# K of the first unit ahead of the query weights on the load queue of a decode attention kernel

## The chip, the core and the metric

The kernel runs on one core of a Trainium2 chip. The metric is the device time of one execution in microseconds: the median of 3 runs of the kernel before is 1936.8 us (1936.79 to 1936.99). The core has TensorE (PE, matmuls; its weight loads are shown as PEld), VectorE (DVE), ScalarE (ACT), GpSimd (POOL) and SyncE (SP), which here does nothing but issue DMAs. The DMAs run on 16 DMA engines. TensorE and the others work on the on-chip memory SBUF; matmul results go to PSUM.

## What is computed

Two attention blocks, A and B, of the same sizes, each with its own inputs; the outputs are put side by side. One query token, batch 2, 32 heads of 192, a cache of 8192 keys, a model width of 640, all in bf16.

```python
B, Sq, D = 2, 1, 640
Hq, Hkv, Sk, Dh = 32, 32, 8192, 192        # rep = 1
q = (x @ wq).reshape(B, Sq, Hq, Dh).transpose(0, 2, 1, 3)
scores = einsum("bhqd,bhkd->bhqk", q, k_cache) * Dh ** -0.5
o = einsum("bhqk,bhkd->bhqd", softmax(scores), v_cache)
out = o.transpose(0, 2, 1, 3).reshape(B, Sq, Hq * Dh) @ wo
# concatenate(A's out, B's out) on the last axis
```

Almost all of the data are the caches: 64 K loads and 64 V loads of 6144 KB each.

## The kernel before

**Units.** A unit u (0 to 63) is a pair of heads of one batch entry; units 0 to 31 are block A, 32 to 63 block B. Partition p holds 128 consecutive cache rows of one head, 64 partitions for each of the two heads, so a K or V load is 128 rows of 48 KB, contiguous in DRAM (`ld_kv`, L262). A unit's work has these steps:
- VectorE multiplies K by the query in four chunks (`dve_mul`, L286, profile line L288, signal `("m", u, c)`);
- TensorE sums groups of products with an identity matrix into PSUM, 12 matmuls a chunk (`pe_sum`, L365, `("s", u, c)`); VectorE reduces the rest (L292);
- the maximum over all partitions goes through GpSimd (L269), the exponential through ScalarE (L327);
- TensorE sums V with the weights, 64 matmuls (`pe_pv`, L379, `("pv", u)`); VectorE and ScalarE normalise.

A product buffer is used by every second chunk, so the multiply of chunk c waits for the sums of chunk c - 2.

**Queries.** Before any unit, the queries of all heads are made: `pe_x` (L348) transposes x, `dve_xbc` (L274) copies it out, and `pe_q` (L357) multiplies it with `wq` in 32 steps of 5 matmuls, a step being one pair of heads of both batch entries: steps 0 to 15 belong to block A, 16 to 31 to block B. Step hp signals `("pq", hp)`; VectorE (L278) and ScalarE (L283) copy its result into `qall` and signal `("qx", hp)` and `("qa", hp)`. L430 and L431 let TensorE wait for a block's whole weight, and for the copies of x, ahead of its first step. Every `dve_mul` waits by L440 for its K load and also for step 31 with its copies.

**Buffers.** One SBUF tile, `big`, holds three load buffers (0, 1, 2) and two product buffers. While the queries are made, its part behind buffer 0 holds the two query weights: block A's begins at buffer 1, block B's ends with the product buffers (L184 to L187). Buffer 0 is free of them. The loads are numbered in the order K0, K1, V0, K2, V1, K3, V2 and so on (L211 to L214), and load i goes into buffer i mod 3.

**The load queue.** All loads are issued by SP, in the order of L489 to L502, on one queue. The first three lines issue, with no wait, block A's query weight in two pieces (`wq_cut`, L206: the first 2048 of 30720 columns, 512 KB, then 7168 KB), both x inputs (2.5 KB each) and block B's query weight (7680 KB). Then come the K and V loads. A load waits until the work on the load three places ahead is over (`done`, L483): for a K load that is the last multiply of its unit, for a V load the weighted sum. Three of them have other gates:

```python
for i, (kind, u) in enumerate(loads):
    w = [done(i - NBUF)]
    if i in (1, 2):
        w = [("pq", PPB * i - 1)]
    S_sp.add(ld_kv(kind, u), waits=w)
```

So K0 waits for nothing, K1 for step 15 (its buffer holds block A's weight) and V0 for step 31. K2 waits for `("m", 0, 3)`, V1 for `("m", 1, 3)`, K3 for `("pv", 0)`, V2 for `("m", 2, 3)`, K4 for `("pv", 1)`. After the last unit the output weights are loaded and multiplied (`pe_out`, L407), and the result is stored.

TensorE runs unit u's sums and then the weighted sum of unit u - 1's V in each round of its main loop; for the first rounds this gives the order sums of unit 0, sums of unit 1, weighted sum of unit 0, sums of unit 2, weighted sum of unit 1.

Of the kernel before, what the change touches and what calls it, by code (L numbers as in the profile page):

```python
# [117 lines left out]
def build_kernel(nc, blocks, out):  # L118
    NBLK = len(blocks)
    B, Hn, Sk, Dh = blocks[0]["k"].shape  # L120
# [8 lines left out]
    DC = D // 128  # L129
# [7 lines left out]
    NBUF = 3  # L137
# [3 lines left out]
    BUFE = T * Dh  # L141
# [5 lines left out]
    with ExitStack() as es:  # L147
# [7 lines left out]
        big = sb("big", [128, NBUF * BUFE + 2 * PRODE], BF16)  # L155
# [38 lines left out]
        S_sp = _Stream("sp", sem("s_sp"), reg)  # L194
# [6 lines left out]
        def dsem(k, n=1):  # L201
            reg[k] = (sem("d_" + "_".join(str(i) for i in k)), 16 * n)

        dsem(("x",), NBLK)
        WQ0 = 2048
        wq_cut = [[(0, WQ0), (WQ0, DC * Hn * Dh)], [(0, DC * Hn * Dh)]]  # L206
        for blk in range(NBLK):
            dsem(("wq", blk), len(wq_cut[blk]))
            dsem(("odone", blk))
# [5 lines left out]
        buf = {}  # L215
        bcount = [0] * NBUF
        for i, (kind, u) in enumerate(loads):
            buf[kind, u] = i % NBUF
            bcount[i % NBUF] += 1
            reg[(kind, u)] = (bsem[i % NBUF], 16 * bcount[i % NBUF])  # L220

        bk, b62, b63 = buf["k", LASTU], buf["v", LASTU - 1], buf["v", LASTU]
# [22 lines left out]
        def dma(out_ap, in_ap, k):  # L245
            s = reg[k][0]
            return lambda eng: eng.dma_start(out_ap, in_ap).then_inc(s, 16)  # L247

        def ld_x(blk):
            return dma(x4[B * blk:B * blk + B, :], blocks[blk]["x"][:, 0, :], ("x",))  # L250

        def ld_wq(blk, n):
            lo, hi = wq_cut[blk][n]
            src = blocks[blk]["wq"].rearrange("(j c) n -> j (c n)", c=DC)
            return dma(big[:, wq_off[blk] + lo:wq_off[blk] + hi], src[:, lo:hi], ("wq", blk))
# [6 lines left out]
        def ld_kv(kind, u):  # L262
            hp, b = u // B, u % B
            blk, h = hp // PPB, 2 * (hp % PPB)
            src = blocks[blk][kind][b, h:h + 2].rearrange("s (p t) d -> (s p) t d", p=64)
            return dma(kv[buf[kind, u]], src, (kind, u))

        def pool_ar(u):
            return lambda eng: eng.partition_all_reduce(mg[u % 3][:], mp[u % 3][:], 128, bass.bass_isa.ReduceOp.max)  # L269
# [213 lines left out]
        def done(i):  # L483
            if i < 0:
                return None
            kind, u = loads[i]
            return ("m", u, NCH - 1) if kind == "k" else ("pv", u)

        ld_wq(0, 0)(nc.sync)  # L489
        S_sp.add(ld_wq(0, 1))  # L490
        for blk in range(NBLK):
            S_sp.add(ld_x(blk))
        S_sp.add(ld_wq(1, 0))
        for i, (kind, u) in enumerate(loads):
            w = [done(i - NBUF)]
            if i in (1, 2):
                w = [("pq", PPB * i - 1)]
            S_sp.add(ld_kv(kind, u), waits=w)
# [70 lines left out]
def bass_concat_heads__gqa_block_cached__mha_block_cached__decode_kernel(  # L569
    nc: bass.Bass,  # L570
    A_x: bass.AP,
    A_k_cache: bass.AP,
    A_v_cache: bass.AP,
    A_wq: bass.AP,
    A_wo: bass.AP,
    B_x: bass.AP,
    B_k_cache: bass.AP,
    B_v_cache: bass.AP,
    B_wq: bass.AP,
    B_wo: bass.AP,  # L580
    out: bass.AP,
):
    blocks = [
        dict(x=A_x, k=A_k_cache, v=A_v_cache, wq=A_wq, wo=A_wo),
        dict(x=B_x, k=B_k_cache, v=B_v_cache, wq=B_wq, wo=B_wo),
    ]
    build_kernel(nc, blocks, out)
# [28 lines left out]
```

## Time and profile before

| | |
|---|---|
| median of 3 runs | 1936.8 us |
| span of the profiled execution | 1935.4 us |
| bytes read from DRAM | 836.77 MB, 432 GB/s over the span |
| TensorE busy | 1501.1 us (78%) |
| VectorE busy | 1122.5 us (58%) |
| mean granted clock of TensorE | 0.956 |

The span goes from the first instruction to the last; the time of a run is longer by what lies around them. The median stands 1.4 us above the span of the profiled execution. In the rows of the timeline, the first number is the start from the beginning of the span, the second the time until the end of the last of the merged instructions, then engine, line, operation, written and read names, shapes and count; in brackets stands how long the engine had been idle and what released it. "SPq" rows are DMA issues; where two are merged in one row the last of them ends with the row. In the DMA rows the last number is the median time from issue to landing. Rows of a stretch give its length, the busy time of PE, PEld, DVE, ACT and POOL with counts, then the granted clock of TensorE (1 is full speed), the busy share of the DMA engines and the rate.

### The profile page before, as it was taken

The page shows a single profiled execution, that of the slowest core. Times are in us where ns is not written, and L with a number is a line of the kernel's source. Part 1 is how long each engine was busy: PE and PEld are TensorE (multiplying, and loading weights), DVE is VectorE, ACT ScalarE, POOL GpSimd, SP SyncE. Part 2 cuts the span into 40 slices and gives each one's busy share as a digit, 9 for nine tenths or more (in the row PEclk, how much of TensorE's full clock was granted, in tenths as well). Part 3 has the DMA queues.
Part 4 walks back from the last instruction along what each step waited for, and adds up shares of the span by engine and source line. Part 5 has one row for each costly group of instructions (what it writes and reads, how often), then busy time and mean ns, then how long its engine had stood idle before and what let it go on. Part 6 is the DMA issues. An engine that isn't in the chain of part 4 may idle for free.

```text
span 1935.4 us, 19060 instructions
## 1 busy us (share of the span) xinstructions
PE 1501.1 (78%) x7728; PEld 730.0 (38%) x7729; DVE 1122.5 (58%) x907; ACT 142.4 (7%) x519; POOL 28.5 (1%) x113
## 2 busy tenths in 40 slices
PE   5788878878878878877877877877877877877878
PEld 2334433433433433433433333433333433433434
DVE  4765565565565565565565565565565565565560
ACT  3100000000000000000000000000000000000000
POOL 0000000000000000000000000000000000000000
PEclk9899999999999999999999999999999999999998
DMA  9999999999999999999999999999999999999999
GB/s 423 424 435 437 431 434 437 432 433 437 436 429 436 437 430 435 436 432 433 437 435 431 436 435 430 436 437 430 435 437 430 434 438 435 430 436 436 429 436 394
DMA packets 19754, 836.91 MB, mean 432 GB/s; under 512 B 2200, under 2 KB 2336, under 8 KB 2720
## 3 DMA queue, kind: packets, MB, share of 16 engines
q1 hardware_dynamic: 19744, 836.78, 99.9%
q8 instruction: 6, 0.10, 0.0%
q14 instruction: 4, 0.03, 0.0%
HBM read 836.77 MB, written 0.01 MB: 432 GB/s over the span
## 4 chain that ended last, share of the span: by engine, by line
DMA 49%; PE 28%; DVE 17%; issue 5%; DVEq 0%; SPq 0%; ACT 0%; ACTq 0%
DMA big<-in_B_k_cache_dram 25%; DMA big<-in_A_k_cache_dram 22%; PE ops L379 18%; DVE big L288 15%; PE scps L365 8%; DVE sc L292 2%; DMA big<-in_B_wo_dram 1%; PE scps L357 1%; DMA xw<-in_B_x_dram 1%; PE outps L357 0%; PE ops L371 0%; DVEq L288 0%; DVE qall L278 0%; SPq L247 0%; PE scps L407 0%
## 5 line engine op out<-in xcount | busy, mean ns | idle before, releaser
L288 DVE TENSOR_TENSOR big<-big,qall 128x6144 bf16<-128x6144 bf16 x256 | 852.8, 3351 | 526.6 <-DMA big<-in_B_k_cache_dram 278.7
L365 PE MATMUL scps<-big,ident 128*128 128x512 bf16 x3072 | 771.8, 408 | 401.1 <-DVE big L288 398.7
L379 PE MATMUL ops<-big,pb 128*34 128x384 bf16 x4096 | 676.8, 326 | 0.0
L365 PEld LDWEIGHTS scps<-big,ident 128*128 128x128 bf16 x3072 | 301.1, 104 | 865.1 <-DVE big L288 491.0
L379 PEld LDWEIGHTS ops<-big,pb 128*34 128x34 bf16 x4096 | 395.5, 98 | 258.7
L292 DVE TENSOR_REDUCE sc<-scps 128x32 f32<-128x512 f32 x256 | 175.8, 687 | 192.5 <-PE scps L365 192.5
L318 ACT ACTIVATE nb<-mg 64x1 f32<-64x1 f32 x128 | 25.8, 201 | 1706.8 <-POOL mg L269 1706.1
L327 ACT ACTIVATE pb<-sc,nb 64x128 bf16<-64x128 f32 x128 | 55.8, 436 | 7.8
L269 POOL PARTITION_ALL_REDUCE mg<-mp x64 | 25.7, 402 | 1857.9 <-DVE mp L298 1857.9
L298 DVE TENSOR_REDUCE mp<-sc 64x1 f32<-64x128 f32 x128 | 35.9, 280 | 8.3
L312 ACT ACTIVATE qall<-o_sum,rc 2x192 f32 (+1 forms) x64 | 29.0, 453 | 20.7 <-DVE o_sum L309 19.1
L309 DVE TENSOR_TENSOR o_sum<-ops,o_hi 2x192 f32<-2x192 f32 x64 | 22.1, 345 | 7.7
L357 PE MATMUL scps<-big,xw 128*128 x120 | 23.2, 351 | 2.2 <-DVE xw L274 2.2
L327 ACT ACTIVATION_READ_ACCUMULATOR pb<-sc,nb 64x1 f32 x128 | 23.7, 185 | 0.0
L306 DVE COPY o_hi<-ops 2x192 f32<-2x192 f32 x64 | 22.3, 349 | 2.0
L303 DVE RECIPROCAL rc<-ops 2x1 f32<-2x1 f32 x64 | 10.0, 156 | 21.3 <-PE ops L379 19.4
L278 DVE CAST qall<-scps 64x192 f32 x48 | 17.0, 355 | 6.5 <-PE scps L357 4.5
L283 ACT ACTIVATE qall<-scps 64x192 f32 x48 | 15.6, 324 | 30.1 <-DVE qall L278 27.8
L348 PE MATMUL oTps<-ident,xw 4*128 4x4 bf16 x5 | 0.4, 178 | 21.7 <-DMA xw<-in_B_x_dram 21.7
L357 PEld LDWEIGHTS scps<-big,xw 128*128 128x128 bf16 x120 | 12.4, 103 | 11.4 <-issue 5.2
L371 PEld LDWEIGHTS ops<-ones,rs 128*2 128x2 f32 x128 | 5.5, 82 | 26.9 <-issue 26.9
L407 PE MATMUL outps<-big,oT 128*2 128x320 bf16 x96 | 9.5, 375 | 5.6 <-DMA big<-in_A_wo_dram 5.6
(36 smaller groups left out, 67.6 us busy)
## 6 DMA issues: line engine op xcount, KB each, us to landing
big<-in_A_k_cache_dram SPq DMA_DIRECT2D x32, 6144.0 KB, 28.9
big<-in_A_v_cache_dram SPq DMA_DIRECT2D x32, 6144.0 KB, 27.9
big<-in_B_k_cache_dram SPq DMA_DIRECT2D x32, 6144.0 KB, 29.4
big<-in_B_v_cache_dram SPq DMA_DIRECT2D x32, 6144.0 KB, 28.2
big<-in_B_wq_dram SPq DMA_DIRECT2D x1, 7680.0 KB, 37.2
big<-in_A_wo_dram SPq DMA_DIRECT2D x1, 7680.0 KB, 30.1
big<-in_A_wq_dram SPq DMA_DIRECT2D x1, 7168.0 KB, 20.2
big<-in_B_wo_dram SPq DMA_DIRECT2D x1, 4640.0 KB, 30.4
```

What stands on the lines that cost most here:

```text
L269: return lambda eng: eng.partition_all_reduce(mg[u % 3][:], mp[u % 3][:], 128, bass.bass_isa.ReduceOp.max)
L288: return lambda eng: eng.tensor_tensor(prod[c % 2], t[:, c * TC:(c + 1) * TC, :], qall[:, S_dve.at(u), :].broadcast_to([128, TC, Dh]), ALU ...
L292: return lambda eng: eng.tensor_reduce(sc[u % 3][:, c * TC:(c + 1) * TC], scps[(u * NCH + c) % 3][:], AXL.X, ALU.add)
L298: ins = eng.tensor_reduce(mp[u % 3][r, s:s + 1], sc[u % 3][r, :], AXL.X, ALU.max)
L306: return lambda eng: eng.tensor_copy(o_hi[:], ops[u % 3][32:34, Dh:QW])
L309: return lambda eng: eng.tensor_tensor(o_sum[:], ops[u % 3][0:2, 0:Dh], o_hi[:], ALU.add)
L312: return lambda eng: eng.activation(qall[0:2, S_act.at(u), :], o_sum[:].unsqueeze(1), ACTF.Identity, scale=rc[u % 3][:])
L318: ins = eng.activation(nb[u % 3][r, :], mg[u % 3][r, s:s + 1], ACTF.Identity, scale=-scale)
L327: ins = eng.activation(dst, sc[u % 3][r, :].rearrange("p (g j a) -> p g a j", j=JB, a=2), ACTF.Exp, bias=nb[u % 3][r, :], scale=scale, acc ...
L357: ins = eng.matmul(qps[hp % NQ][:, 0:QW], xbc[:, blk, c, :], wq_t[blk][:, c, S_pe.at(off, QW, QW)], start=(c == 0), stop=(c == DC - 1))
L365: ins = eng.matmul(scps[(u * NCH + c) % 3][:], ident[:], prod[c % 2][:, :, j * DG:(j + 1) * DG], start=(j == 0), stop=(j == NJ - 1))
L379: ins = eng.matmul(ops[u % 3][0:MP, 0:QW], pb[u % 3][:, j0s:j0s + MP], vv[:, j, :], start=(j == 0), stop=(j == TJ - 1))
```

## The change

The queue's first entries get another order. K0 now goes out first, in two pieces (columns 0 to 2047 and 2048 to 24575 of each partition's row: 512 KB and 5632 KB) by a new function `ld_k0`; then both x loads; then block A's query weight, whole; then block B's, whole. The loop over the loads leaves out entry 0. Buffers, gates of all other loads, and all work on the engines stay as they are. The semaphore of buffer 0 counts K0 as two transfers.

```diff
-        WQ0 = 2048
-        wq_cut = [[(0, WQ0), (WQ0, DC * Hn * Dh)], [(0, DC * Hn * Dh)]]
+        wq_cut = [[(0, DC * Hn * Dh)], [(0, DC * Hn * Dh)]]
+        k_cut = [(0, 2048), (2048, BUFE)]
...
-            bcount[i % NBUF] += 1
+            bcount[i % NBUF] += len(k_cut) if i == 0 else 1
...
+        def ld_k0(n):
+            lo, hi = k_cut[n]
+            src = blocks[0]["k"][0, 0:2].rearrange("s (p t) d -> (s p) (t d)", p=64)
+            return dma(big[:, lo:hi], src[:, lo:hi], ("k", 0))
...
-        ld_wq(0, 0)(nc.sync)
-        S_sp.add(ld_wq(0, 1))
+        assert buf["k", 0] == 0
+        ld_k0(0)(nc.sync)
+        S_sp.add(ld_k0(1))
         for blk in range(NBLK):
             S_sp.add(ld_x(blk))
+        S_sp.add(ld_wq(0, 0))
         S_sp.add(ld_wq(1, 0))
         for i, (kind, u) in enumerate(loads):
+            if i == 0:
+                continue
             w = [done(i - NBUF)]
```

## The prediction

> **What bounds the kernel now.** I read the DMA rows of the page first, then the busy sums.
>
> ```profile
> span 1935.4 us, 19060 instructions
> PE 1501.1 (78%) x7728; PEld 730.0 (38%) x7729; DVE 1122.5 (58%) x907; ACT 142.4 (7%) x519; POOL 28.5 (1%) x113
> DMA  9999999999999999999999999999999999999999
> GB/s 423 424 435 437 431 434 437 432 433 437 436 429 436 437 430 435 436 432 433 437 435 431 436 435 430 436 437 430 435 437 430 434 438 435 430 436 436 429 436 394
> q1 hardware_dynamic: 19744, 836.78, 99.9%
> ```
>
> The 16 DMA engines are busy 99.9% of the span, and the rate is flat. The kernel is one stream of bytes: a microsecond in which the queue is empty is lost for good, and compute costs nothing as long as it gives buffers back in time. By the busy sums, a unit (one of 64) takes 1501.1 / 64 = 23.5 us of TensorE and 17.5 of VectorE. Next, the rate by stretches (columns: length, busy time of PE, PEld, DVE, ACT, POOL, clock, DMA share, GB/s):
>
> ```profile
> 54.10:98.77 44.67, 32.77 (x139) 14.08 (x140) 32.60 (x21) 3.53 (x15) 3.78 (x2) 0.89 0.99 430
> 98.77:127.96 29.19, 25.52 (x139) 12.79 (x136) 17.15 (x14) 1.85 (x7) 0.35 (x1) 1.00 1.02 439
> 300.00:1900.00 1600.00, 1250.45 (x6365) 606.21 (x6363) 942.61 (x718) 102.61 (x387) 19.49 (x55) 0.96 1.00 434
> ```
>
> At 434 GB/s a K or V load (6144 KB, 6.29 MB) takes 14.5 us, so a unit's two take 29.0, some 5 us more than its TensorE work. A lag of compute therefore heals by about 5 us a unit, but what the stream lost before it healed stays lost. So the change must be judged by when each early load is issued against when the load ahead of it ends. These are the issue rows, the times to landing (last number), and, from the view of the issuing line, the largest time to landing:
>
> ```profile
> 0.72 0.88 SPq L247 DMA_DIRECT2D big<-in_A_wq_dram  x2
> 2.30 0.36 SPq L247 DMA_DIRECT2D big<-in_B_wq_dram  x1
> 2.70 37.84 SPq L247 DMA_DIRECT2D big<-in_A_k_cache_dram  x2
> 53.34 0.33 SPq L247 DMA_DIRECT2D big<-in_A_v_cache_dram  x1
> 71.82 0.33 SPq L247 DMA_DIRECT2D big<-in_A_k_cache_dram  x1
> 89.26 0.33 SPq L247 DMA_DIRECT2D big<-in_A_v_cache_dram  x1
> 102.71 0.33 SPq L247 DMA_DIRECT2D big<-in_A_k_cache_dram  x1
> 113.26 0.33 SPq L247 DMA_DIRECT2D big<-in_A_v_cache_dram  x1
> ```
> ```profile
> big<-in_B_wq_dram SPq DMA_DIRECT2D x1, 7680.0 KB, 37.2
> big<-in_A_wq_dram SPq DMA_DIRECT2D x1, 7168.0 KB, 20.2
> big<-in_A_wq_dram SPq DMA_DIRECT2D x1, 512.0 KB, 3.7
> DMA to landing us min/median/max: 3.7/30.3/51.3
> ```
>
> The second weight lands at 2.30 + 37.2 = 39.5. The 51.3 can only be K of unit 0, issued at 2.70 behind everything else: it lands at 54.0, 14.5 after the weight. K of unit 1 follows in the queue, then V0 (53.34), K2 (71.82), V1 (89.26), K3 (102.71), V2 (113.26). The compute side of that stretch:
>
> ```profile
> 24.29 4.98 PE L357 MATMUL scps<-big,xw 128*128 x15 [2.18 <-DVE xw L274]
> 39.20 0.98 PE L357 MATMUL outps<-big,xw 128*128 x5
> 52.34 0.98 PE L357 MATMUL outps<-big,xw 128*128 x5
> 58.65 7.96 PE L365 MATMUL scps<-big,ident 128*128 128x512 bf16 x24 [5.33 <-DVE big L288]
> 102.61 5.61 PE L365 MATMUL scps<-big,ident 128*128 128x512 bf16 x24
> ```
> ```profile
> 55.19 6.63 DVE L288 TENSOR_TENSOR big<-big,qall 128x6144 bf16<-128x6144 bf16 x2 [0.99 <-ACT qall L283]
> 85.89 3.35 DVE L288 TENSOR_TENSOR big<-big,qall 128x6144 bf16<-128x6144 bf16 x1
> 98.77 6.62 DVE L288 TENSOR_TENSOR big<-big,qall 128x6144 bf16<-128x6144 bf16 x2 [5.38 <-DMA big<-in_A_k_cache_dram]
> 127.96 6.63 DVE L288 TENSOR_TENSOR big<-big,qall 128x6144 bf16<-128x6144 bf16 x2 [9.62 <-DMA big<-in_A_k_cache_dram]
> 156.89 6.63 DVE L288 TENSOR_TENSOR big<-big,qall 128x6144 bf16<-128x6144 bf16 x2 [7.68 <-DMA big<-in_A_k_cache_dram]
> ```
>
> Projections run on TensorE from 24.29 without a gap: block A's end at 40.18, block B's at 53.32. The first score multiply starts at 55.19, released by the last query copy, 1.2 us after K0 landed. Units 0 and 1 then run as fast as compute allows (85.89 + 3.35 = 89.24, and V1 goes out at 89.26). At 98.77 VectorE waits for K2's data for the first time, and from there DMA leads.
>
> **The change, part by part.** All rates below are those of these rows.
>
> *The bytes.* The same six transfers go out at the start, in another order. Two go first as pieces and the merged weight saves one, so SP's issue time stays (0.88 us for two). The first piece is 512 KB as before. I cost this at nothing; the stream has no hole to remove there, so a gain is excluded but for the first fill, which the equal first piece keeps. Either way it is below the 0.4 us of one issue.
>
> *The x loads* move behind K0's 14.5 us instead of behind the first weight, so they land around 18 instead of 21.7 (the first row of the next fence), and the transposition and copies up to 24.29 are over some 15 us before a weight is there. That removes 24.29 - 21.4 = 2.9 us (the first weight landed near 1.2 + 20.2) from between weight and projections. Nothing is gained by it, since the second weight sets what follows.
>
> *The second weight* now ends where K0 ended: 54.0. This is the cost. No multiply may start before the last projection (the waits of L440), so K0, there from about 17 us, lies idle. The first weight lands at 21.4 + 14.5 = 35.9; block A's projections take 40.18 - 24.29 = 15.9 us from a cold start, so they end near 51.85. TensorE then waits 2.2 us, starts again at 54.05 and needs 53.32 - 40.18 = 13.1 us at full clock. Does that wait cool the clock?
>
> ```profile
> 21.75 0.35 PE L348 MATMUL oTps<-ident,xw 4*128 4x4 bf16 x5 [21.75 <-DMA xw<-in_B_x_dram]
> 76.92 7.04 PE L365 MATMUL scps<-big,ident 128*128 128x512 bf16 x24 [2.31 <-DVE mp L298]
> 149.75 7.80 PE L379 MATMUL ops<-big,pb 128*34 128x384 bf16 x47
> 160.31 6.65 PE L365 MATMUL scps<-big,ident 128*128 128x512 bf16 x24 [2.76 <-DVE big L288]
> 168.42 2.76 PE L365 MATMUL scps<-big,ident 128*128 128x512 bf16 x12 [1.46 <-DVE big L288]
> 76.90:79.00 2.10, 2.08 (x7) 0.85 (x8) 2.10 (x1) 0.00 (x0) 1.95 (x1) 0.68 1.25 542
> ```
>
> Twenty-four matmuls without a gap took 5.61 us (102.61). After gaps of 2.76 and 2.31 us they took 6.65 and 7.04, so 1.0 and 1.4 more, and the granted clock behind the second was 0.68; after 1.46 us twelve took 2.76, nothing more. The bounds for a gap of 2.2 are 0 and 1.4. I take 1.0, from the gap that follows an unbroken stream (149.75 to 157.55), as here. So the last projection ends at 54.05 + 13.1 + 1.0 = 68.2 instead of 53.32: **compute starts 14.9 us later**, the first multiply near 70.1.
>
> The Trainium skill, "TensorE: Matmul & The Clock Gate", section "What's actually happening", lets the clock fall to half only after an idle window of about 3.4 us; by that a wait of 2.2 us costs nothing. The rows at 76.92 and 160.31 disagree for gaps shorter than that.
>
> *What the shift meets.* Four loads wait for it, and SP issues in order, so each also holds all behind it. An issue into an empty queue lands after a fixed part and its own 14.5: the fixed part is 3.7 us less 1.2 us for 0.52 MB at 434, so 2.5; I keep 1.5 to 3.5 open, since only this one transfer shows it. A load that finds the queue full lands 14.5 after the one ahead.
> - K1 (waits for block A's projections): 51.85 + 17.0 = 68.85, against 54.0 + 14.5 = 68.5 with a full queue. A pause of 0.35.
> - V0 (block B's): 68.2 + 17.0 = 85.2. Before it was 98.77 - 14.5 = 84.3, so 0.9 late.
> - K2 (unit 0's last multiply): 71.82 + 14.9 = 86.7, landing at 103.7, against 98.77: 4.9 late.
> - V1 (unit 1's last multiply): 89.26 + 14.9 = 104.2, landing at 121.2, against 98.77 + 14.5 = 113.3: **7.9 late**.
> - K3 (unit 0's weighted sum): 102.71 + 14.9 + 17.0 = 134.6, but the queue gives 121.2 + 14.5 = 135.7. No new pause.
> - V2: 113.26 + 14.9 + 17.0 = 145.2, against 135.7 + 14.5 = 150.2. None, and the margin grows from here.
>
> These are not added: each holds the earlier ones. The loss is that of V1, that is the shift of 14.9 less the 98.77 - 2.5 - 89.26 = 7.0 us by which V1 was early. Everything after rides on the stream, to the end. Sum: span 1935.4 + 7.9 = 1943.3; the runs' median is 1936.8, 1.4 above the span, so **1944.7 us**.
>
> The same chain can be shorter by what cold clock it holds. Its first 24 matmuls took 7.96 after 5.33 us of idleness, its next 7.04: at most 2.35 + 1.4 = 3.8 of the 34 us, if both were warm. With no cooling of the projections either, the loss is 3.1. The other end: cooling as long as after 5.33 us (2.35) and a fixed part of 3.5 give 7.9 + 1.35 + 1.0 = 10.3.
>
> **The rivals.**
> - *The clock holds through the 2.2 us.* Then the shift is 13.9, the loss 6.9 and the time 1943.7. For it: the gap is a little shorter than any that cooled. Against: 2.31 cooled. This is the result of the skill's rule above.
> - *Only the direct gates count.* If the multiplies of units 0 and 1 make up the delay (a chain of 30 us rather than 34, warm throughout, and a fixed part below 2.5), only V0 is late: 0.9 to 3 us, 1937.7 to 1940. Against: the 5.33 us ahead of the first score sums is the last copies plus a multiply, which the change leaves there.
> - *The stream makes it up, so the kernel is not slower.* The stretch from 98.77 ran at 439 GB/s right after one at 430. If the engines could hold 439, then 8 us would be regained at 5/434 in some 700 us, and the end would stand at 1936.8. It decides from unit 3 on: K would have to land every 28.6 us instead of 29.0. Against: in 1600 us with loads always queued the mean stayed 434.
> - *The lag goes on.* If K3 and V2 also find the queue empty, the loss tends to the whole shift: 1936.8 + 14.9 = 1951.7. Against: a margin of 1.1 us at K3 and 5 at V2.
> - *The change doesn't do what it says:* if multiplies of unit 0 could start on their own query, K0 early would be of use and only V0's 0.9 us would be lost, 1937.7. The trace can't exclude it, because K0's landing and the last copy fall 1 us apart; the list of waits in the code does.
>
> **How the numbers follow.** Cooled clock, 1944.7: 0.48. Warm, 1943.7: 0.25. Lag goes on: 0.09. Only direct gates: 0.08. Made up: 0.07. Not what it says: 0.03. A measurement of this kernel tells a change from none at about 0.2%, 3.9 us. The first three are slower by more than that, and of the direct gates, 0.02: 0.84. Of the made-up case I give 0.04 to faster, since a rate of 439 need not stop at what was lost; the remaining 0.12 is within 0.2%. The range takes the losses from 4.2 to 10.8 us, 1941.0 to 1947.6; below it are the two cases near 1937 and the faster one, above it most of the lasting lag.
>
> **What would show it.** The x matmuls near 18 us and the first projection near 36; a TensorE gap of about 2 us near 52 and a half clock behind it; the first multiply near 70.1; K2 issued near 86.7 and V1 near 104.2; GB/s in the second and third slice down by about 10% and 6%, and the other slices as they are; later K landings 29.0 apart and 7.9 late (156.89 becomes 164.8). A first multiply before 60 would make the whole sum wrong; a first multiply near 70 without the late landings would break the step from shift to loss; rates above 434 later on would bring in the third rival.

## The result and the profile after

| | before | changed |
|---|---|---|
| median of the runs | 1936.89 us (4 runs, 1936.79 to 1937.14) | 1945.92 us (4 runs, 1944.07 to 1947.07) |
| span of the profiled execution | 1935.4 us | 1942.6 us |
| spread of the runs | 0.35 us | 3.0 us |

The ratio is 1.0046 (95% interval 1.0033 to 1.0058): 9.0 us slower at the median, and 7.2 us by the spans of the two profiled executions. The profiled execution of the changed kernel is its fastest run. The prediction was 1944.7, with a range of 1941.0 to 1947.6.

First the page of the changed kernel: span, DMA share and rate in 40 slices, and the load queue.

```profile
span 1942.6 us, 19081 instructions
DMA  9999999999999999999999999999999999999999
GB/s 413 394 419 433 431 435 437 432 430 435 435 434 434 431 435 435 434 434 431 434 436 433 435 430 434 436 434 434 430 435 436 433 433 432 434 437 433 433 432 390
q1 hardware_dynamic: 19744, 836.78, 99.7%
```

The digit row shows nothing: the pauses are too short for a slice of 49 us. The rates show them. The second and third slices fell from 424 and 435 to 394 and 419, by 7% and 4% where about 10% and 6% were forecast. The first fell too, from 423 to 413; it is 413 in e1 below as well, which has the old order, so this does not come from the order. The other slices stay within 7 GB/s. Next the issue rows of the changed kernel (K1, V0, K2, V1, K3), and from the view of the DMA issues, taken for each load alone, the time from issue to landing (last number; in order block B's weight, issued at 2.70, then K1, V0, K2, V1).

```profile
52.50 0.33 SPq L247 DMA_DIRECT2D big<-in_A_k_cache_dram  x1
67.86 0.33 SPq L247 DMA_DIRECT2D big<-in_A_v_cache_dram  x1
85.44 0.33 SPq L247 DMA_DIRECT2D big<-in_A_k_cache_dram  x1
101.64 0.33 SPq L247 DMA_DIRECT2D big<-in_A_v_cache_dram  x1
115.09 0.33 SPq L247 DMA_DIRECT2D big<-in_A_k_cache_dram  x1
```
```profile
big<-in_B_wq_dram SPq DMA_DIRECT2D x1, 7680.0 KB, 51.4
...
big<-in_A_k_cache_dram SPq DMA_DIRECT2D x1, 6144.0 KB, 17.8
...
big<-in_A_v_cache_dram SPq DMA_DIRECT2D x1, 6144.0 KB, 20.2
...
big<-in_A_k_cache_dram SPq DMA_DIRECT2D x1, 6144.0 KB, 19.2
...
big<-in_A_v_cache_dram SPq DMA_DIRECT2D x1, 6144.0 KB, 18.1
```

The second weight lands at 2.70 + 51.4 = 54.1. K1, V0, K2 and V1 all go out only 1.6 to 3.0 us before the load ahead of them lands, with the queue nearly empty, and land at 70.3, 88.1, 104.6 and 119.7. The same view of the kernel before, for K2 (issued 71.82) and V1 (issued 89.26):

```profile
big<-in_A_k_cache_dram SPq DMA_DIRECT2D x1, 6144.0 KB, 26.9
...
big<-in_A_v_cache_dram SPq DMA_DIRECT2D x1, 6144.0 KB, 24.0
```

There K2 landed at 98.7 and V1 at 113.3, so V1 is 6.5 us late in the changed kernel's fastest run. TensorE and VectorE of the changed kernel in the head, the stretch up to the first units:

```profile
18.14 0.35 PE L353 MATMUL oTps<-ident,xw 4*128 4x4 bf16 x5 [18.14 <-DMA xw<-in_B_x_dram]
36.34 4.98 PE L362 MATMUL scps<-big,xw 128*128 x15 [17.85 <-DMA big<-in_A_wq_dram]
51.49 0.98 PE L362 MATMUL outps<-big,xw 128*128 x5
54.48 2.61 PE L362 MATMUL scps<-big,xw 128*128 x15 [2.01 <-ACT qall L288]
66.86 0.98 PE L362 MATMUL outps<-big,xw 128*128 x5
73.17 6.98 PE L370 MATMUL scps<-big,ident 128*128 128x512 bf16 x24 [5.33 <-DVE big L293]
90.55 2.76 PE L370 MATMUL scps<-big,ident 128*128 128x512 bf16 x12 [2.31 <-DVE mp L303]
```
```profile
69.71 6.63 DVE L293 TENSOR_TENSOR big<-big,qall 128x6144 bf16<-128x6144 bf16 x2 [0.99 <-ACT qall L288]
98.26 3.35 DVE L293 TENSOR_TENSOR big<-big,qall 128x6144 bf16<-128x6144 bf16 x1
105.80 6.63 DVE L293 TENSOR_TENSOR big<-big,qall 128x6144 bf16<-128x6144 bf16 x2
134.28 6.63 DVE L293 TENSOR_TENSOR big<-big,qall 128x6144 bf16<-128x6144 bf16 x2 [3.57 <-DMA big<-in_A_k_cache_dram]
163.53 6.63 DVE L293 TENSOR_TENSOR big<-big,qall 128x6144 bf16<-128x6144 bf16 x2 [8.81 <-DMA big<-in_A_k_cache_dram]
```

Here K0 lies ready while TensorE waits 17.85 us for the first weight and 2.01 us ahead of block B's projections (the row names ScalarE, but what came last was the second weight, at 54.1); the first multiply starts at 69.71 instead of 55.19. VectorE is the late one through unit 2 (no DMA wait at 105.80), and K3 at 134.28 is the first load it waits for again. From there the stream leads, 6.3 us behind that of before (127.96), and K4 at 163.53 is 6.6 behind.

### The profile page after: what moved, and what is told of

Same layout as the page of the kernel before. It is cut to its first block, busy times and chain, and to the rows that moved or that the text cites. A ratio compares the mean times of both kernels' runs of the same rounds, so it can differ in the third digit from the quotient of the medians.

```text
span 1942.6 us, 19081 instructions
## 1 busy us (share of the span) xinstructions
PE 1533.7 (79%) x7729; PEld 738.9 (38%) x7729; DVE 1123.0 (58%) x907; ACT 142.3 (7%) x519; POOL 31.6 (2%) x113
## 4 chain that ended last, share of the span: by engine, by line
DMA 47%; PE 32%; DVE 17%; issue 3%; DVEq 0%; SPq 0%; ACT 0%; ACTq 0%
DMA big<-in_B_k_cache_dram 24%; DMA big<-in_A_k_cache_dram 21%; PE ops L384 18%; DVE big L293 15%; PE scps L370 12%; DMA big<-in_A_wq_dram 2%; DVE sc L297 1%; DMA big<-in_B_wo_dram 1%; PE scps L362 1%; PE outps L362 0%; PE ops L376 0%; DVE qall L283 0%; DVEq L293 0%; SPq L247 0%; PE scps L412 0%
## 5 line engine op out<-in xcount | busy, mean ns | idle before, releaser
L370 PE MATMUL scps<-big,ident 128*128 128x512 bf16 x3072 | 804.1, 421 | 362.3 <-DVE big L293 360.0
L370 PEld LDWEIGHTS scps<-big,ident 128*128 128x128 bf16 x3072 | 310.2, 106 | 849.4 <-DVE big L293 446.5
L303 DVE TENSOR_REDUCE mp<-sc 64x1 f32<-64x128 f32 x128 | 35.9, 281 | 8.3
L353 PE MATMUL oTps<-ident,xw 4*128 4x4 bf16 x5 | 0.4, 178 | 18.1 <-DMA xw<-in_B_x_dram 18.1
## 6 DMA issues: line engine op xcount, KB each, us to landing
big<-in_B_wq_dram SPq DMA_DIRECT2D x1, 7680.0 KB, 51.4
```

The costliest lines, as they stand in the source:

```text
L303: ins = eng.tensor_reduce(mp[u % 3][r, s:s + 1], sc[u % 3][r, :], AXL.X, ALU.max)
L370: ins = eng.matmul(scps[(u * NCH + c) % 3][:], ident[:], prod[c % 2][:, :, j * DG:(j + 1) * DG], start=(j == 0), stop=(j == NJ - 1))
```

## The experiments

All diffs are against the changed kernel unless another is named; their code is shortened, and a line of several loads gives the order of issue. Times are medians with the range of the runs; the kernel before, run beside them on the same chip, stood at 1936.78 to 1936.85.

**The pieces without the new order (e1).**

```diff
-ld_k0(0), ld_k0(1), ld_x(0), ld_x(1), ld_wq(0), ld_wq(1)
+ld_wq(0), ld_x(0), ld_x(1), ld_wq(1), ld_k0(0), ld_k0(1)
```

> Queue order of before (block A's weight, x, block B's weight, K0), but with the changed kernel's pieces: block A's weight whole, K0 in 512 KB and 5632 KB. Theory (the late second weight is the cost, the pieces are free): within 0.4 us of the 1936.9 of before, runs within 0.5 us of each other. Rival (the cut of K0 or the whole first weight costs something of its own): above 1938.

1937.52 us (1937.23 to 1937.69, 11 runs) against 1936.81 (1936.54 to 1937.13, 15 runs of the kernel before). Neither expectation held: the order makes nearly all of the loss, but the pieces cost 0.7 us, and the two sets of runs do not overlap. Two more runs share it out.

**One piece at a time (f1, f2), each against the kernel before.**

```diff
 # f1
-wq_cut = [[(0, WQ0), (WQ0, DC * Hn * Dh)], [(0, DC * Hn * Dh)]]
+wq_cut = [[(0, DC * Hn * Dh)], [(0, DC * Hn * Dh)]]
 # f2
-K0 whole, as ld_kv
+ld_k0(0), ld_k0(1), behind both weights
```

> The kernel before with one thing changed: block A's query weight goes out whole instead of in two pieces; K0 stays whole and last. It and f2_k0_cut share out the 0.7 us by which e1_cut_only, which has both, was slower than before. If the whole weight is what costs (a first transfer that fills the empty queue later, or another state of the queue's end): 1937.4 to 1937.7. If not: within 0.25 us of before.

> The kernel before with one thing changed: K0 goes out in two pieces, at its old place behind both weights. If the cut of K0 is what costs the 0.7 us of e1_cut_only: 1937.4 to 1937.7. If not: within 0.25 us of before.

1937.32 (1937.21 to 1937.51) and 1937.11 (1936.97 to 1937.23), against 1936.78: 0.5 and 0.3 us. Both fall short of the 1937.4 expected of a piece that costs the whole 0.7, and both lie beyond the 0.25 of one that costs nothing, so each has some share. The time isn't lost in the head. V1 lands at 113.3 in e1 as before, and the two traces part in the last microseconds, at the last loads of the output weights. The last row of such matmuls, of the kernel before and then of e1:

```profile
1932.15 1.44 PE L407 MATMUL scps<-big,oT 128*2 128x320 bf16 x16 [0.19 <-DMA big<-in_B_wo_dram]
```
```profile
1932.69 1.47 PE L412 MATMUL scps<-big,oT 128*2 128x320 bf16 x16 [0.59 <-DMA big<-in_B_wo_dram]
```

TensorE waits 0.59 us instead of 0.19 for the last bytes. That the cuts leave the 16 engines finishing at more uneven times is a guess; no run shows it.

**The first weight ahead of K0 (e2).**

```diff
-ld_k0(0), ld_k0(1), ld_x(0), ld_x(1), ld_wq(0), ld_wq(1)
+ld_wq(0), ld_x(0), ld_x(1), ld_k0(0), ld_k0(1), ld_wq(1)
```

> Block A's weight first, then x, then K0 in its two pieces, then block B's weight. Block A's projections end near 40 as before and K1 is issued then; the second weight still lands at 54. Theory (only the second weight's landing counts): as slow as the changed kernel or slower, 1944 to 1948, since TensorE now waits about 14 us ahead of block B's projections and starts them at half clock (some 2 us more than after the 2 us gap); V1 is issued between 101 and 106. Rival (K1's late issue, or K0 ahead of everything, is the cost): 1937 to 1938.

1948.85 us (1947.43 to 1949.21, 5 runs), ratio 1.0062 (1.0049 to 1.0076): even slower than the changed kernel, and 0.85 us above the expected 1944 to 1948. TensorE and SP of e2:

```profile
55.05 4.28 PE L362 MATMUL scps<-big,xw 128*128 x15 [16.11 <-DMA big<-in_B_wq_dram]
```
```profile
38.97 0.33 SPq L247 DMA_DIRECT2D big<-in_A_k_cache_dram  x1
105.02 0.33 SPq L247 DMA_DIRECT2D big<-in_A_v_cache_dram  x1
```

K1 goes out at 38.97, 13.5 us sooner than in the changed kernel, and it is of no use, nor is it K0's place ahead of the first weight that costs. Block B's weight still comes behind K0, V1 still goes out late, at 105.02, and after the long wait the projections start at half clock (15 matmuls in 4.28 us instead of 2.61).

**x ahead of everything (e4).** Both x loads first, then as in the changed kernel.

> The changed kernel with both x loads at the head of the queue, ahead of K0. Theory: x is early enough in either place, so the time is that of the changed kernel, 1944 to 1947; the x matmuls move from 18 us to below 6. Rival (the place of the x loads behind K0 matters): below 1943 or above 1948.

1947.94 us (1946.25 to 1948.28, 5 runs). The x matmuls start at 2.92 instead of 18.14, and nothing is gained. The median lies 0.9 us above the expected 1944 to 1947, and just short of the rival's 1948. Part of that is the start of the stream: K0's first piece now goes out at 1.40 instead of 0.72, and the second weight lands at 54.7 instead of 54.1.

**How much may go ahead (d1, d2, d3).** Only the first n columns of K0 go ahead; the rest follows block B's weight.

```diff
-k_cut = [(0, 2048), (2048, BUFE)]
+k_cut = [(0, n), (n, BUFE)]          # n = 6144, 12288, 18432 of 24576
-ld_k0(0), ld_k0(1), ld_x(0), ld_x(1), ld_wq(0), ld_wq(1)
+ld_k0(0), ld_x(0), ld_x(1), ld_wq(0), ld_wq(1), ld_k0(1)
```

> Only the first quarter of K0 (1536 KB, 3.6 us) goes ahead of x and the weights; the rest of K0 follows block B's weight. Theory (threshold: compute shifts by the bytes ahead of the second weight, and the first 6 to 7 us of the shift are free): 1936.9, runs within 0.5 us. Rival (the loss is in proportion to the bytes moved ahead): 1939.1.

> The first half of K0 (3072 KB, 7.25 us) goes ahead, the rest follows block B's weight. Theory (threshold of 6 to 7 us): 1937.1 to 1938.5, the clock's phase in the head adding up to 1 us. Rival (in proportion): 1941.4.

> Three quarters of K0 (4608 KB, 10.9 us) go ahead, the rest follows block B's weight. Theory (threshold of 6 to 7 us, then microsecond for microsecond): 1940.5 to 1943, runs spread over 2 to 3 us. Rival (in proportion): 1943.7.

| ahead of the second weight | median (range) | V1 issued, landed, span in the profiled run |
|---|---|---|
| nothing (before) | 1936.8 (1936.6 to 1937.1) | 89.26, 113.3, 1935.4 |
| a quarter (d1) | 1937.34 (1937.13 to 1940.21, 10 runs) | 91.32, 113.1, 1935.9 |
| half (d2) | 1941.75 (1937.55 to 1942.50, 10 runs) | 97.92, 116.5, 1938.5 |
| three quarters (d3) | 1944.01 (1943.55 to 1946.08, 5 runs) | 101.91, 120.1, 1943.0 |
| all (changed) | 1945.92 (1944.07 to 1947.07, 4 runs) | 101.64, 119.7, 1942.6 |

By their medians alone these runs don't settle it. The median of a quarter speaks for the threshold, though three of its ten runs took 1938.8 to 1940.2 where all were expected within 0.5 us; half and three quarters came out by the rival's numbers, not by mine. The traces show what the time hangs on: every span follows V1's landing (span less landing is 1822.0 to 1822.9 in all five, and 1821.8 to 1822.9 in the traces of all the other runs of this section), and the landing follows the issue once this is later than about 95. Two runs of ten of d2 have a loss of only 0.7 us (1937.55 and 1937.58), and the others 3.2 to 5.7; a loss in proportion to the bytes would not come and go. What comes and goes is taken up next.

**The clock in the head (e3, e5, and r1 for comparison).** Matmuls whose results nobody reads are added on TensorE to fill its idle stretches: ahead of the projections, between the two blocks', ahead of the sums of unit 0 and of unit 1. No other work is changed.

```diff
+put("pe", PQ0 - 1, 0, pe_warm(NW[0]), ...)             # 68 in e3, 62 in e5
+put("pe", PQ0 + PPB - 0.75, 0, pe_warm(NW[1]), ...)    # 12, 21
+put("pe", 0, -0.5, pe_warm(NW[2]), ...)                # 20, 20
+put("pe", 0, 0.35, pe_warm(NW[3]), ...)                # 8, 8
```

> The changed kernel with 108 matmuls added on TensorE, whose results nobody reads: 68 ahead of the projections, 12 between the two blocks' projections, 20 ahead of unit 0's sums, 8 ahead of unit 1's, so that its clock does not fall in the head. Theory (the compute chain up to unit 1's last multiply sets the loss, and the clock's phase in it makes the runs spread over 3 us): V1 issued near 100 instead of 101.6, time 1942.3 (1941.5 to 1943.2), runs within 0.8 us. Rival (the spread comes from how the DMA engines restart after the pause): 1944 to 1947 and a spread of some 3 us, as in the changed kernel.

> The changed kernel with added matmuls as in e3_warm, but 21 instead of 12 between the two blocks' projections, so that TensorE has less than 1 us without work ahead of block B's weight (62, 21, 20 and 8 in all, from another tile). Theory (clock phases in the head explain both the spread and what the median has above the profiled run): block B's projections at full clock, V0 issued near 68.5, V1 near 101, landing near 119; 1942.5 to 1944, runs within 1.2 us. Rival (something else in the stream, as the late V1 of e3_warm hints): 1944.5 to 1947 as before.

> The changed kernel unaltered, for its spread beside the two that follow. All theories: 1944 to 1948, median near 1946.

The changed kernel again: 1946.50 (1945.88 to 1948.76). e3: 1945.59 (1944.76 to 1946.83). e5: 1944.92 (1944.28 to 1946.02), 5 runs each. TensorE of r1, at two of its cooled places, and of e5 (whose trace lacks one record of the 21 matmuls between the blocks):

```profile
54.38 4.12 PE L362 MATMUL scps<-big,xw 128*128 x15 [2.94 <-DMA big<-in_B_wq_dram]
91.88 6.89 PE L370 MATMUL scps<-big,ident 128*128 128x512 bf16 x24 [2.31 <-DVE mp L303]
```
```profile
49.64 4.70 PE L471 MATMUL ops<-xw,ident 128*128 128x512 bf16 x20
55.48 2.61 PE L362 MATMUL scps<-big,xw 128*128 x15 [1.15 <-DMA big<-in_B_wq_dram]
74.19 2.76 PE L370 MATMUL scps<-big,ident 128*128 128x512 bf16 x12 [0.97 <-DVE big L293]
90.27 2.76 PE L370 MATMUL scps<-big,ident 128*128 128x512 bf16 x12 [0.59 <-DVE mp L303]
```

In e3 the twelve matmuls between the blocks were too few: TensorE still waited 2.89 us, and the first 15 projection matmuls behind it took 4.29 us, with the granted clock at 0.50 for most of them. In e5 the granted clock is 1.00 from the first projection to V1's issue, and V1 goes out at 101.37 instead of r1's 104.07. That is 2.7 us, but only 1.6 of them reach the median, and the range of the five runs is 1.7 us against 2.9 and not below 1.2. The reason is in V1's row, of r1 and then of e5:

```profile
big<-in_A_v_cache_dram SPq DMA_DIRECT2D x1, 6144.0 KB, 18.1
```
```profile
big<-in_A_v_cache_dram SPq DMA_DIRECT2D x1, 6144.0 KB, 20.2
```

V1 of e5 took 2.1 us longer, so it lands only 0.6 us sooner (121.6 against 122.2). Most of the other 1.0 us between these two traces, each taken in the median run of its five, comes at the very end, where TensorE waits 0.69 and 0.62 us for the last output weights in r1, and 0 and 0.31 in e5. The issue times came as the theory expected, near 101 in e5; the times did not. Both medians lie in the range that the rival gave, 1944 to 1947 and 1944.5 to 1947, so something in the stream takes back most of what the clock gives. What that is stays open (last section). Five runs each are too few to say that the spread fell.

**Half of K0 ahead, with a warm head (d4).** As d2, with 58, 21, 20 and 8 such matmuls.

> d2_half (half of K0 ahead) with such added matmuls: 58 ahead of the projections, 21 between the blocks, 20 and 8 ahead of the sums of units 0 and 1. Theory (a threshold: V1 is free as long as it is issued before 95): V0 near 61, V1 near 93.5, so the loss of d2_half is gone, 1936.9 to 1937.7, runs within 0.6 us. Rival (a loss in proportion to the bytes ahead): 1941 to 1942 as d2_half.

1937.87 us (1937.38 to 1938.10, 11 runs), against 1941.75 (1937.55 to 1942.50) of d2 with the same bytes ahead. SP of d2 and of d4, the issue of V1:

```profile
97.92 0.33 SPq L247 DMA_DIRECT2D big<-in_A_v_cache_dram  x1
```
```profile
94.44 0.33 SPq L247 DMA_DIRECT2D big<-in_A_v_cache_dram  x1
```

This settles it against the rival in proportion to the bytes. With the transfers and their order unchanged, the loss falls from 4.9 us to 1.0 by the medians, and the range of the runs from 5.0 us to 0.7. In the two traces, V1 goes out 3.5 us sooner and the span falls by 1.9, from 1938.5 to 1936.6; the profiled run of d2 was one of its quicker ones, 1.7 below its median. Of the 1.2 us that are left in the span of d4, 0.9 is V1's landing, at 114.2 instead of 113.3 though it went out at 94.44, before 95; V0 and K2 were 0.7 and 0.5 late already. So the limit of 95 is not exact, and the expectation, whose range the median passes by 0.2 us, left this out.

## Why the prediction was right

**The bound and the mechanism held.** The kernel is one stream of bytes. The second weight behind K0 shifts all compute, the shift eats the head start of the early loads (the time by which each was issued sooner than it needed to be), and what is left over is lost for good. Point by point:

- *The second weight lands at 54.0*: 54.1. *The x matmuls near 18*: 18.14, without use, as e4 shows too. *The first projection near 36*: 36.34.
- *K1, V0 and K2 late, V1 the latest, K3 and V2 free*: so it was, but V0 landed 3.8 us late (67.86 + 20.2 = 88.1, against 53.34 + 30.9 = 84.2) where 0.9 was forecast. K3 landed 14.6 us after V1 (115.09 + 19.2 = 134.3, against 119.7), the time of a full queue, and V2 14.6 after K3.
- *V1 issued at 104.2, landed at 121.2*: 101.64 and 119.7 in the fastest run, 104.07 and 122.2 in r1. The issue is met by r1 to 0.1 us.
- *Rates as before later on*: 434 GB/s from 300 to 1900 us in the changed kernel, as this row of its stretches shows. The rival that the stream makes it up falls, and with it the only way to a faster kernel. That of the direct gates falls too: from V0's issue to V1's, compute made up 2.1 of the 14.5 us by which V0 went out later.

```profile
300.00:1900.00 1600.00, 1286.26 (x6295) 615.38 (x6294) 942.52 (x715) 102.40 (x388) 19.49 (x55) 0.93 1.00 434
```

Five terms were mis-sized; the last of them is hidden in the sum:

- *The fixed part of a transfer into an empty queue*: I took 2.5 from a 512 KB transfer and kept 1.5 to 3.5 open. V1 shows 18.1 - 14.5 = 3.6, just outside. V1's head start was therefore 98.7 + 14.5 - 18.1 - 89.26 = 5.8 us and not 7.0. This is the limit of about 95 in the table above.
- *The cooled clock*: I took 1.0 us. From the second weight's landing to V0's issue it is 67.86 - 54.1 = 13.8 us in the profiled run, which kept full clock through its gap of 2.01 us, and 69.09 - 54.0 = 15.1 in r1, which did not: 1.3 us, near the upper bound of 1.4. Even at full clock it was 13.8 and not the 13.1 of the sum.
- *The chain from V0's issue to V1's*, carried over unchanged at 35.9 us, took 33.8 in the profiled run and 35.0 in r1. The prediction named the cold clock in it as what could shorten it, but put that at nothing in the sum.
- *The pieces*, costed at nothing, take 0.7 us at the end of the kernel (e1).
- *A load into a nearly empty queue.* The sum takes the later of two times, 17.0 after the issue or 14.5 after the load ahead. V0 kept neither: it landed 20.2 after its issue and 17.8 after K1. This is hidden, since V1 was later still, but not by much in the fastest run: K2 was already 5.9 us late there, V1 6.5. In r1 it is 5.7 and 8.9.

The errors have opposite signs, and that the forecast lies 1.2 us from the median owes something to luck: in the profiled run V1's issue came 2.6 us sooner than forecast, its head start was 1.2 smaller, and the pieces added 0.7.

With the measured terms the two profiled runs come out, in part by construction, since the 18.1 is theirs. Fastest run: V1 is 101.64 - 89.26 = 12.4 us later, less 5.8 is 6.6, plus 0.7 is 7.3, against 7.2 of the spans. r1: 14.8 - 5.8 + 0.7 = 9.7, against 1945.0 - 1935.4 = 9.6. The same sum gives the spans of e2, e4 and d3 to 0.2 us, and that of d2 0.5 too high; in e3 and e5, where V1 took over 20 us to land, it is 1.5 and 1.0 too low.

**The rival of the warm clock** (1943.7) is what the profiled run did ahead of block B's projections, at 1944.07. So the two likeliest cases are not alternatives for the kernel; its runs can fall in one or the other, as these two traces do. The chain from V0's issue to V1's took 33.8 us in that run, 35.0 in r1 and 35.9 before. The same gap of 2.31 us ahead of unit 1 left the clock alone in the one (12 sums in 2.76 us) and cooled it in r1 (24 in 6.89 instead of 5.35 without a gap). Together these phases make the 2.4 us between the issues of V1 in the two traces, and the spans differ by as much. Before, such differences fell inside V1's head start: over the traces of the kernel before, e1, f1 and f2, V1's issue varies from 87.12 to 89.26 and its landing only from 113.1 to 113.3. That goes far to explain why the kernel before repeats to 0.35 us and the changed one only to 3; e5 says that the clock is not the whole of it.

The Trainium skill, "TensorE: Matmul & The Clock Gate", section "What's actually happening", has a free-running activity window of about 3.4 us and half clock after an idle one. The free run agrees with the two outcomes of the 2.31 us gap; the need for a whole idle window doesn't, since gaps of 2.31 and 2.94 us (r1) and 2.13 us (e4) cooled it.

## What to carry to other kernels

In a kernel like this one, where DMA is busy all the time, reordering loads did not gain by itself: it only changed when buffers came free. Work out for each early load how long before the end of the load ahead it is issued, and compare the delay of its gate with that; only the excess is lost, but it is lost for good, and a chain that was slack becomes a bound with all its variation. An operand that cannot be used before another has arrived does not belong ahead of it on the queue.

## What the runs showed of the hardware that was not expected

- A 6144 KB load issued within 0.8 us of the landing of the load ahead, before or after it, lands 17.4 to 18.6 us after its issue (V1 of r1, issued at 104.07, 0.3 us before K2 landed: 18.1; V0 of e3, 0.7 us after K1: 17.4; V0 of e2, 0.8 us after K1: 18.6), 2.9 to 4.1 us over the 14.5 of a full queue.
- A load issued 1 to 3 us before the one ahead lands can be later than both rules give. V1 of e5 was issued 2.2 us before K2 landed (85.17 + 18.4 = 103.6) and landed 18.0 us after it; V0 of the changed kernel, 2.4 us before, landed 17.8 after; V1 of the changed kernel, 3.0 us before, landed 15.1 after. K2 of d2, as much as 4.1 us before, landed 15.8 after. Whether the 16 engines restart unevenly was not tried, and it stays open, like the second weight's landing at 55.1 instead of 54.1 in e3 and e5.
- TensorE's clock fell after a gap of 2.13 us (e4, the row below: 15 projection matmuls in 3.74 us instead of 2.61) and held through one of 2.01 us (the row at 54.48).

```profile
55.02 3.74 PE L362 MATMUL scps<-big,xw 128*128 x15 [2.13 <-DMA big<-in_B_wq_dram]
```
